# An attention kernel with a feed-forward behind it: the end of the sixth pair moved up, the first feed-forward begun five beats sooner, keys in blocks of 112

## The chip, the cores and the metric

The kernel runs on one core of a Trainium2 chip. The metric is the device time of one execution in microseconds. The median of three runs of the kernel before is 1040.24 us (1039.77 to 1040.38).

## The reference

Eight batches, twelve heads, 448 tokens, head size 64, all float32. Each head is normalised, attends over its 448 keys, and the heads of a token laid side by side (768 numbers) go through a feed-forward whose hidden layer is the largest of three products.

```
q_n = q / sqrt(mean(q*q) + 1e-6) * g_q          (k_n the same with g_k)
attn = softmax(q_n @ k_n.T / 8)
x = (attn @ v), heads side by side: 3584 x 768
h = max(x @ w1, x @ w2, x @ w3)                  768 x 768 each
out = h @ w_out                                  3584 x 768
```

## The kernel before, in words

Two heads make a pair, six pairs a batch, 48 pairs in all (numbered from 0 here, so that the sixth pair is pair 5). A pair has four chunks of queries: three of 128 rows for both heads, and a fourth of 64 rows for each head, which fill one PSUM bank together. So a pair has seven banks of scores.

**Two ways of doing a pair.** Pairs 0 to 5, all of batch 0, are done in float32 (`PLAIN = 6`): TensorE turns the exponentials by transposes against an identity (`turn_plain`, L627), ScalarE copies them out of PSUM (`keep_turned`), and the products with the values follow (`add_values`, L739). The sums of the softmax are turned and spread by sixteen small matmuls (`spread_sums`), copied by `keep_sums`, and the result is scaled by `scale_plain` and cut into two float16 parts by `finish`. From pair 6 on each number is two float16 parts; the weights of the softmax are cut by `upper_weights` (ScalarE, VectorE) and `lower_weights` (VectorE), and DMA does the turning (`turn_weights`).

**The order of the work is written out by hand.** A pair has twelve beats, and `beat(g, i)` (L993) issues what belongs to beat i while pair g is in its softmax. "Beat 6.4" is beat 4 of pair 6 in this text. Every engine does its instructions in the order of issue. While pair g is in its softmax, the end of the pair before (w = g - 1) is done: its sums, its products with the values, and `finish`. `later(n, work)` puts work off by n beats, to the end of that beat. Chunk c of a pair begins at beat 3c; from pair 6 on the scores of the next chunk are issued at beat 3c + 2, and VectorE's row maximum of a chunk stands ahead of `lower_weights` of the chunk before it.

**The feed-forward** of a batch is a generator (`ffn`, L874) of steps: a step of the first layer is three matmuls of 448 columns (L788), 108 of them a batch; a step of the second is three matmuls of 384 columns (L850), 36 or 48 a batch. `thirds` (L901) draws some two steps a beat, 24 a pair, from a queue of batches. Batch 0 enters the queue at beat 6.6, after its last pair; of its first two units only the first five of six steps are drawn at first, since the sixth needs the sixth pair. Later batches enter at beat 10 of the pair that follows them. If the queue is empty, no feed-forward is drawn.

**The weights** come as float32 in 24 blocks (18 of the first layer, 6 of the second). `prep_block` makes them ready: ScalarE works on the raw block (L186), VectorE takes three instructions (L194, L198, L203). A block of the first layer is due every 4 beats, one of the second every 8 (`BLOCK_BEATS`, L33); the next raw block of the second layer is loaded 9 beats after the block two ahead of it was begun.

**PSUM**: two buffers of two banks for scores, one bank for the products with the values, three banks (`ps_m`) that the turned tiles, the spread sums and the sums of the feed-forward share.

Of the kernel before, what the change touches and what calls it, by code (L numbers as in the profile page):

```python
# [13 lines left out]
ALU = mybir.AluOpType  # L14
AX = mybir.AxisListType.X

P = 128
# [12 lines left out]
LEAST = 2.0 ** -60  # L30


BLOCK_BEATS = (4, 8)  # L33


PLAIN = 6
# [6 lines left out]
def qknorm_attention_maxout_ffn_kernel(  # L43
# [35 lines left out]
    nc = tc.nc  # L79
    B, H, S, D = q.shape  # L80
    DM, DF = w1.shape
    DO = w_out.shape[1]
    NP = H // 2
# [5 lines left out]
    NH = 2  # L89
    HW = DO // NH  # L90
    LEFT = S - 3 * P
    G = B * NP
    HALVES = (slice(0, 64), slice(64, 128))
    TERMS = ((0, 0), (0, 1), (1, 0))
# [33 lines left out]
    ident = const.tile([P, P], F32, name="ident")  # L128
# [3 lines left out]
    ones_c = const.tile([P, 1], F32, name="ones_c")  # L132
# [34 lines left out]
    def row_largest(dst, src):  # L167
        nc.vector.tensor_reduce(dst, src, axis=AX, op=ALU.max, apply_absolute_value=True)
# [178 lines left out]
    v_tiles = {}  # L347

    def load_v(t):

        b, n = divmod(t, 2)
        vr = sb.tile([P, NP, 4, D], F32, name="vr", bufs=3)
        rows = v[b, NP * n:NP * (n + 1)]
        for u in range(3):
            nc.sync.dma_start(
                out=vr[:, :, u],
                in_=rows[:, u * P:(u + 1) * P].rearrange("h p d -> p h d"),
            )
        for half, part in zip(HALVES, (rows[:, 3 * P:S], rows[:, 0:LEFT])):
            nc.sync.dma_start(out=vr[half, :, 3], in_=part.rearrange("h p d -> p h d"))  # L360
        v_tiles[t] = vr

    def values_of(g):
        return v_tiles[g // 3][:, 2 * (g % 3):2 * (g % 3) + 2]
# [88 lines left out]
    def turn_whole(g, what):  # L453
# [10 lines left out]
        for to, of, rows in (  # L464
            (slice(0, LEFT), last, upper),
            (slice(LEFT + 3 * P, 512), last, lower),
# [22 lines left out]
    v_rows = {}  # L489
# [3 lines left out]
    def largest_v(t):  # L493
        b, n = divmod(t, 2)
        if b not in v_rows:
            v_rows[b] = sb.tile([P, 2], F32, name="v_rows", bufs=2)
        row_largest(
            v_rows[b][:, n:n + 1], v_tiles[t].rearrange("p h n d -> p (h n d)")
        )

    def bound_v(b):
        most = sb.tile([P, 1], F32, name="v_most", bufs=2)
        nc.vector.tensor_reduce(most, v_rows.pop(b), axis=AX, op=ALU.max)

        box = []


        def spread():
            box.append(ps_m.tile([P, 512], F32, name="most", tag="m"))
            nc.tensor.matmul(  # L510
                box[0][:, 0:1], ones_c.broadcast_to([P, P]), most, start=True, stop=True
            )

        def scale():
            nc.vector.tensor_scalar(
                out=v_down[:, b:b + 1], in0=box[0][:, 0:1], scalar1=LEAST, scalar2=1.0 / UP,
                op0=ALU.max, op1=ALU.mult,
            )
            nc.vector.reciprocal(v_up[:, b:b + 1], v_down[:, b:b + 1])

        later(2, spread)
        later(3, scale)
# [104 lines left out]
    def turn_plain(g, c):  # L627
        s = st[g]
        e = s.pop(("e", c))
        if c == 0:  # L630
            s["pt"] = sb.tile([P, 14, 512], F16, name="pt", bufs=2)
        s["turned"] = []
        s.pop(("sc", c))
        for h in range(banks(c)):
            turned = ps_m.tile([P, 512], F32, name="turned", tag="m")
            for u in range(3):
                block = e[:, h, u * P:(u + 1) * P]
                nc.tensor.transpose(turned[:, u * P:(u + 1) * P], block, ident)
            for first, rows in ((S - P, P), (S - LEFT, LEFT)):
                nc.tensor.transpose(turned[:rows, 3 * P:], e[:, h, first:S], ident)  # L640
            s["turned"].append(turned)

    def keep_turned(g, c):
        s = st[g]
        pt = pt_plain(s)
        turned = [t.rearrange("p (u q) -> p u q", u=4) for t in s.pop("turned")]
        for h in range(2):
            if c < 3:
                first = LEFT * h + c * P
                nc.scalar.copy(pt[:, h, :, first:first + P], turned[h])  # L650
            else:
                first = 0 if h else 3 * P
                nc.scalar.copy(
                    pt[:, h, :, first:first + LEFT], turned[0][:, :, HALVES[h]]
                )


# [81 lines left out]
    def add_values(g):  # L739
        s = st[g]  # L740
        av = ps_a.tile([P, 512], F32, name="av", tag="a")
        s["av"] = av
        if g < PLAIN:
            vr, pt = values_of(g), pt_plain(s)
            for u in range(4):
                rows = HALVES[0] if u == 3 else slice(0, P)
                for h, half in enumerate(HALVES):
                    nc.tensor.matmul(
                        av[half, :S], vr[rows, h, u], pt[rows, h, u],
                        start=u == 0, stop=u == 3,  # L750
                    )
            return
        vp, vs, pt = s["vp"], s["vs"], s["pt"]
        steps = [(part, u, u) for u in range(4) for part in range(2)]
        steps += [(2, u, 4 + u) for u in range(3)]
        for n, (part, u, block) in enumerate(steps):
            for h, half in enumerate(HALVES):
                values = vs[:, h, u] if part == 2 else vp[:, part, 4 * h + u]
                nc.tensor.matmul(  # L759
                    av[half, :S], values, pt[:, 7 * h + block, SHIFT[h]:SHIFT[h] + S],  # L760
                    start=n == 0, stop=n == len(steps) - 1,
                )
# [152 lines left out]
    for i, src in enumerate((g_q, g_k)):  # L915
        nc.scalar.dma_start(
            out=gains[:, i], in_=src.rearrange("(o d) -> o d", o=1).broadcast_to([P, D])
# [75 lines left out]
    def beat(g, i):  # L993
        w, n = g - 1, g + 2
# [19 lines left out]
        if part == 2:  # L1014
            if early:
                row_max(*divmod(k + 1, 4))
            elif k + 1 < 4 * G:
                scores(*divmod(k + 1, 4))
        if 0 <= w < PLAIN:
            if i == 1:  # L1020
                guard_sums(w)
            if i == 2:
                inverse_sums(w)
            if i == 5:
                spread_sums(w)
            if i == 6:
                keep_sums(w)
            if i == (8 if w < PLAIN else 9):
                scale_plain(w)
        if w >= 0 and i == (4 if w < PLAIN else 7):  # L1030
            add_values(w)
        thirds(THIRDS[i] + (len(queue) > 1 and i % 6 == 4))
        if w >= 0 and i == (9 if w < PLAIN else 10):
            finish(w, x_of[w // NP])
        if w >= 0 and g % NP == 0 and i == (6 if w < PLAIN else 10):
            queue.append(ffn(w // NP, x_of[w // NP]))

        if g + 1 < G:
# [55 lines left out]
        n_in = min(decoded[0], NFT * NJ)  # L1094
        due_at = BLOCK_BEATS[0] * n_in + BLOCK_BEATS[1] * (decoded[0] - n_in)
        if decoded[0] < len(blocks) and clock[0] > due_at:
# [44 lines left out]
```

## Time and profile before

| | before |
|---|---|
| median of three runs | 1040.24 us |
| the profiled execution | 1039.46 us |
| its span, first to last instruction | 1037.6 us |
| TensorE (PE) busy | 985.4 us, 95% |
| VectorE (DVE) busy | 709.3 us, 68% |
| ScalarE (ACT) busy | 637.1 us, 61% |
| GpSimd (POOL) busy | 614.2 us, 59% |
| mean granted TensorE clock | 0.984 of full speed |

The profile is of one execution. The shares of busy time are averages over stages that differ: the first 134 us (pairs 0 to 5), a stage in which the feed-forward sets in (to about 160 us), and the long rest. A stage's own rows say what it waits for. In a timeline row a bracket gives the idle time of the engine before the row and the work that ended it.

### The profile page before, as it was taken

To read this page: it belongs to the slowest core of one execution; us is meant where nothing else is said; L and a number is where in the kernel's file an instruction comes from. 1 tells how busy PE (TensorE), PEld (TensorE's weight loads), DVE (VectorE), ACT (ScalarE), POOL (GpSimd) and SP (SyncE) were. 2 spreads that over 40 slices of the span, in tenths; PEclk is the share of its full clock that TensorE was granted. 3 is DMA by queue.
4 is the path that set the end of the run, shared out by engine and by line. 5 is a ranking of instruction groups with operands and counts; after the bars stand their busy time and mean duration, and the time that the engine had idled before them with its cause. 6 is when DMAs were issued, how large, how long until landed. Compare 5 with 4: busy or idle time off the path is not lost.

```text
span 1037.6 us, 17168 instructions
## 1 busy us (share of the span) xinstructions
PE 985.4 (95%) x5850; PEld 527.5 (51%) x5850; DVE 709.3 (68%) x1316; ACT 637.1 (61%) x1437; POOL 614.2 (59%) x661
## 2 busy tenths in 40 slices
PE   5889869997899999999999999999999999999998
PEld 3555434444445555555555555555555555555555
DVE  4999989898676766777667757676677757760120
ACT  3697877757756666666666676666665766651111
POOL 5567878875766765767656666666675766400000
PEclk9899979999999999999999999999999999999999
DMA  7756669998999999999999899999999898762001
GB/s 176 190 159 170 158 162 205 186 177 139 211 180 176 164 185 204 172 176 155 211 169 185 156 202 196 175 169 182 191 172 174 168 202 148 139 99 62 1 1 61
DMA packets 524887, 166.17 MB, mean 160 GB/s; under 512 B 501120, under 2 KB 520576, under 8 KB 524800
## 3 DMA queue, kind: packets, MB, share of 16 engines
q1 hardware_dynamic: 461792, 149.09, 74.3%
q10 hardware_dynamic: 63008, 16.00, 8.8%
q8 instruction: 46, 0.75, 0.3%
q14 instruction: 41, 0.34, 0.1%
HBM read 53.54 MB, written 11.01 MB: 62 GB/s over the span
## 4 chain that ended last, share of the span: by engine, by line
PE 50%; DMA 1%; ACT 0%; SPq 0%; DVE 0%; issue 0%
PE acc L788 29%; PE acc L850 10%; PE av L759 5%; PE sc L579 5%; PE sc L586 1%; DMA pt<-pp 0%; DMA out_dram<-osb 0%; ACT osb L859 0%; SPq L732 0%; PE most L510 0%; DVE rs L700 0%; DVE rs L696 0%
## 5 line engine op out<-in xcount | busy, mean ns | idle before, releaser
L788 PE MATMUL acc<-xt,w_sb 128*128 128x448 f16 x2592 | 513.2, 353 | 0.0
L788 PEld LDWEIGHTS <-w_sb 128*128 128x128 f16 x2592 | 251.2, 98 | 242.7 <-issue 12.2
L617 ACT ACTIVATE sc<-sc,nm 128x448 f32<-128x448 f32 x294 | 178.8, 608 | 189.5 <-DVE nm L601 185.0
L601 DVE TENSOR_REDUCE nm<-sc 128x2 f32<-128x896 f32 x192 | 186.4, 971 | 97.8 <-PE sc L586 51.7
L703 ACT ACTIVATE pp<-sc,rs 128x448 f16<-128x448 f32 x294 | 172.8, 633 | 78.1 <-ACT sc L617 29.2
L713 DVE SCALAR_TENSOR_TENSOR pp<-sc,rs,pp 128x448 f16<-128x448 f32 x294 | 188.0, 675 | 4.9 <-ACT pp L703 4.9
L395 POOL TENSOR_TENSOR ri<-ri,half_neg 128x7 f32<-128x7 f32 x96 | 146.1, 1522 | 8.0
L850 PE MATMUL acc<-wo_sb,ht 128*128 128x384 f16 x864 | 147.9, 327 | 0.0
L429 POOL TENSOR_TENSOR kp<-kn,kp 128x448 f16<-128x448 f32 x42 | 44.3, 1056 | 168.6 <-ACT kp L423 159.0
L579 PE MATMUL sc<-kt,qt 128*128 128x448 f16 x504 | 117.5, 356 | 16.1 <-DVE pp L713 12.2
L850 PEld LDWEIGHTS <-ht 128*128 128x128 f16 x864 | 83.5, 98 | 59.6 <-issue 4.7
L579 PEld LDWEIGHTS <-qt 128*128 128x128 f16 x504 | 48.8, 98 | 63.6 <-issue 11.1
L759 PE MATMUL av<-pt,vp 128*64 128x448 f16 x672 | 72.6, 356 | 2.3 <-DMA pt<-pp 2.1
L817 POOL COPY hx<-ht 128x128 f16<-128x128 f16 x48 | 13.9, 289 | 93.6 <-DVE ht L812 89.3
L381 DVE TENSOR_REDUCE ss<-sq 128x7 f32<-128x448 f32 x96 | 57.7, 602 | 11.3 <-ACT sq L372 8.1
L541 POOL TENSOR_TENSOR vp<-vr,vp 128x512 f16<-128x512 f32 x42 | 49.9, 1189 | 22.6 <-ACT vp L535 22.6
L696 DVE TENSOR_SCALAR rs<-sc 128x2 f32<-128x2 f32 (+1 forms) x168 | 26.3, 157 | 52.5 <-ACT sc L617 52.5
L774 DVE SCALAR_TENSOR_TENSOR xt<-av,xt 128x448 f16<-128x448 f32 x42 | 26.2, 623 | 48.5 <-ACT xt L773 48.5
L802 DVE TENSOR_TENSOR m<-acc,m 128x448 f32<-128x448 f32 x48 | 29.6, 617 | 37.7 <-PE acc L788 37.5
L429 POOL TENSOR_TENSOR qp<-qn,qp 128x448 f16<-128x448 f32 x42 | 43.5, 1035 | 19.0 <-ACT qp L423 17.1
L759 PEld LDWEIGHTS <-vp 128*64 128x64 f16 x672 | 35.4, 109 | 36.6 <-issue 17.6
L808 ACT ACTIVATE ht<-acc 128x448 f16<-128x448 f32 x48 | 26.2, 546 | 41.8 <-DVE acc L802 41.8
(126 smaller groups left out, 1235.5 us busy)
## 6 DMA issues: line engine op xcount, KB each, us to landing
raw<-in_moe_w_dram SPq DMA_DIRECT2D x18, 768.0 KB, 4.6
kt<-kt SPq DMA_DIRECT2D x84, 112.0 KB, 2.4
vr<-in_v_dram SPq DMA_DIRECT2D x48, 192.0 KB, 4.2
out_dram<-osb SPq DMA_DIRECT2D x24, 384.0 KB, 3.4
kr<-in_k_dram ACTq DMA_DIRECT2D x34, 224.0 KB, 3.2
qr<-in_q_dram ACTq DMA_DIRECT2D x34, 224.0 KB, 4.5
raw<-in_moe_w_out_dram SPq DMA_DIRECT2D x6, 768.0 KB, 5.6
vs<-vp SPq DMA_DIRECT2D x84, 48.0 KB, 2.0
```

What stands on the lines that cost most here:

```text
L381: nc.vector.tensor_reduce(sums[g % 2][:, KQ[what]], sq, axis=AX, op=ALU.add)
L395: nc.gpsimd.tensor_tensor(out=ri, in0=ri, in1=half_neg[:, at], op=ALU.pow)
L429: nc.gpsimd.tensor_tensor(out=parts[:, :, 1], in0=n, in1=parts[:, :, 0], op=ALU.subtract)
L541: nc.gpsimd.tensor_tensor(out=vp[:, 1], in0=values_of(g).rearrange("p h n d -> p (h n) d"), in1=vp[:, 0], op=ALU.subtract,)
L579: nc.tensor.matmul(sc[:, h, :S], qt[:, 4 * h + c], kt[:, n, keys[h]], start=n == 0, stop=n == 1,)
L601: nc.vector.tensor_reduce(nm[:, :n], sc[:, :n, :S], axis=AX, op=ALU.max, negate=True)
L617: nc.scalar.activation(to, sc[:, h, :S], AF.Exp, bias=nm[:, h:h + 1], accum_out=total,)
L703: nc.scalar.activation(pp[:, h, 0], sc[:, h, :S], AF.Copy, scale=rs[:, h:h + 1])
L713: nc.vector.scalar_tensor_tensor(out=pp[:, h, 1], in0=sc[:, h, :S], scalar=rs[:, h:h + 1], in1=pp[:, h, 0], op0=ALU.mult, op1=ALU.subtract,)
L759: nc.tensor.matmul(av[half, :S], values, pt[:, 7 * h + block, SHIFT[h]:SHIFT[h] + S], start=n == 0, stop=n == len(steps) - 1,)
L788: nc.tensor.matmul(acc[:, :S], wt[:, wp, c], xs[c][:, xp], start=(c == 0 and n == 0), stop=(c == NCT - 1 and n == 2),)
L850: nc.tensor.matmul(acc[:, :HW], lhs, wo_sb[:, f, wp, half * HW:(half + 1) * HW], start=(f == 0 and n == 0), stop=(f == NFT - 1 and n == 2),)
```

## The change

The kernel after differs in three things.

- **Keys in blocks of 112** for batch 0: the 448 keys are four blocks of 112 instead of three of 128 and one of 64. A bank of exponentials is turned by four transposes instead of five; values of batch 0 are loaded in four transfers of 112 rows instead of five; the products with the values contract over 112 rows four times instead of 128 three times and 64 once.
- **The end of the sixth pair**, which is done in pair 6, is moved up: guarding the sums from beat 1 to 0, inverting them from 2 to 1, spreading them from 5 to 2, keeping them from 6 to 3, the products with the values from 4 to 2 (behind the spreading), scaling from 8 to 4, `finish` from 9 to 5. The other pairs keep their beats.
- **Batch 0 enters the feed-forward's queue** at beat 6.1 instead of 6.6, and blocks of the second layer are due every 7 beats instead of 8.

```
-BLOCK_BEATS = (4, 8)
+BLOCK_BEATS = (4, 7)
...
+    KEYS = S // 4
...
+        if b == 0:
+            for u in range(4):
+                nc.sync.dma_start(
+                    out=vr[:KEYS, :, u],
+                    in_=rows[:, u * KEYS:(u + 1) * KEYS].rearrange("h p d -> p h d"),
+                )
+            return
...
-            for u in range(3):
-                block = e[:, h, u * P:(u + 1) * P]
-                nc.tensor.transpose(turned[:, u * P:(u + 1) * P], block, ident)
-            for first, rows in ((S - P, P), (S - LEFT, LEFT)):
-                nc.tensor.transpose(turned[:rows, 3 * P:], e[:, h, first:S], ident)
+            for u in range(4):
+                nc.tensor.transpose(
+                    turned[:KEYS, u * P:(u + 1) * P], e[:, h, u * KEYS:(u + 1) * KEYS],
+                    ident,
+                )
...
-                rows = HALVES[0] if u == 3 else slice(0, P)
                 for h, half in enumerate(HALVES):
                     nc.tensor.matmul(
-                        av[half, :S], vr[rows, h, u], pt[rows, h, u],
+                        av[half, :S], vr[:KEYS, h, u], pt[:KEYS, h, u],
...
+        ends = w >= 0 and g % NP == 0
+        guard, spread, add, scale, end = (
+            (1, 5, 4, 8, 9) if w < PLAIN - 1 else (0, 2, 2, 4, 5) if w < PLAIN
+            else (0, 0, 7, 0, 10)
+        )
         if 0 <= w < PLAIN:
-            if i == 1:
+            if i == guard:
                 guard_sums(w)
-            if i == 2:
+            if i == guard + 1:
                 inverse_sums(w)
-            if i == 5:
+            if i == spread:
                 spread_sums(w)
-            if i == 6:
+            if i == spread + 1:
                 keep_sums(w)
-            if i == (8 if w < PLAIN else 9):
+            if i == scale:
                 scale_plain(w)
-        if w >= 0 and i == (4 if w < PLAIN else 7):
+        if w >= 0 and i == add:
             add_values(w)
         thirds(THIRDS[i] + (len(queue) > 1 and i % 6 == 4))
-        if w >= 0 and i == (9 if w < PLAIN else 10):
+        if w >= 0 and i == end:
             finish(w, x_of[w // NP])
-        if w >= 0 and g % NP == 0 and i == (6 if w < PLAIN else 10):
+        if ends and i == (1 if w < PLAIN else 10):
             queue.append(ffn(w // NP, x_of[w // NP]))
```

The reductions over the values of batch 0 and the copies of the turned tiles are cut to 112 partitions as well.

## Rows read from the trace of the kernel before

**Rows 1.** Page, part 1: engine, busy us (share of the span), instructions.

```profile
PE 985.4 (95%) x5850; PEld 527.5 (51%) x5850; DVE 709.3 (68%) x1316; ACT 637.1 (61%) x1437; POOL 614.2 (59%) x661
```

**Rows 2.** Chain that ended last, in order of time: start, us, what.

```profile
519.63 4.08 PE acc L788 x21
523.71 0.76 PE sc L579 x4
```

**Rows 3.** Windows, 10 us: length, busy (instructions) by engine, PEclk, DMA, GB/s.

```profile
110.00:120.00 10.00, 6.13 (x29) 3.54 (x29) 9.90 (x13) 8.88 (x20) 8.87 (x7) 0.83 0.68 162
...
130.00:140.00 10.00, 4.98 (x23) 3.18 (x23) 6.43 (x13) 8.48 (x20) 8.26 (x7) 0.83 0.62 161
...
140.00:150.00 10.00, 6.85 (x29) 3.64 (x25) 9.93 (x17) 5.33 (x10) 8.27 (x8) 0.69 0.74 170
```

**Rows 4.** Window of 18.6 us, one pair long, in the long rest.

```profile
310.97:329.57 18.60, 18.60 (x112) 9.52 (x110) 13.35 (x27) 12.51 (x30) 11.92 (x16) 1.00 1.02 170
```

**Rows 5.** Timeline of PE, two banks turned: start, us, line, tile, count.

```profile
117.44 0.90 PE L638 MATMUL turned<-ident,e 128*128 128x128 f32 x3
...
118.56 0.84 PE L638 MATMUL turned<-ident,e 128*128 128x128 f32 x3
```

**Rows 6.** Waits of VectorE, 20 to 140 us: total us, times, longest.

```profile
DVE top L156 <- PE marks L153: 2.3, 2, 1.4
```

**Rows 7.** Timeline of PE, pair 6 up to the first scores of pair 7.

```profile
138.29 0.35 PE L510 MATMUL most<-v_most,ones_c 128*128 128x1 f32 x2 [1.69 <-ACT qp L423]
...
138.57 3.57 PE L748 MATMUL av<-pt,vr 128*64 128x448 f32 x16
...
145.29 1.65 PE L579 MATMUL sc<-kt,qt 128*128 128x448 f16 x4 [3.15 <-DVE pp L713]
...
146.87 1.54 PE L673 MATMUL spread<-ident,sum 128*64 128x128 f32 x6
...
152.03 5.16 PE L788 MATMUL acc<-xt,w_sb 128*128 128x448 f16 x21
...
157.03 0.92 PE L579 MATMUL sc<-kt,qt 128*128 128x448 f16 x4
```

**Rows 8.** Timeline of PE, pair 5: first and last of four spreading groups.

```profile
123.16 0.87 PE L673 MATMUL spread<-ident,sum 128*64 128x128 f32 x6
...
125.01 0.32 PE L679 MATMUL spread<-ident,sum 64*64 64x64 f32 x2
```

**Rows 9.** Timeline of VectorE, pair 6.

```profile
139.91 0.20 DVE L664 RECIPROCAL sum<-sum 128x7 f32<-128x7 f32 x1 [0.67 <-ACT sum L660]
...
143.97 1.26 DVE L713 SCALAR_TENSOR_TENSOR pp<-sc,rs,pp 128x448 f16<-128x448 f32 x2
```

**Rows 10.** Timeline of PE, pair 12: scores of its chunks, then of pair 13.

```profile
263.96 0.92 PE L579 MATMUL sc<-kt,qt 128*128 128x448 f16 x4
...
268.62 0.92 PE L579 MATMUL sc<-kt,qt 128*128 128x448 f16 x4
...
272.44 0.92 PE L579 MATMUL sc<-kt,qt 128*128 128x448 f16 x4
...
275.73 0.57 PE L586 MATMUL sc<-kt,qt 128*64 128x448 f16 x4 [0.17 <-DVE pp L713]
...
278.95 0.92 PE L579 MATMUL sc<-kt,qt 128*128 128x448 f16 x4 [2.65 <-ACT sc L617]
```

**Rows 11.** Windows of 1 us.

```profile
144.00:145.00 1.00, 0.00 (x0) 0.00 (x0) 1.00 (x3) 0.88 (x3) 0.92 (x3) 0.50 0.85 172
...
277.00:278.00 1.00, 0.00 (x0) 0.00 (x0) 0.43 (x1) 1.00 (x4) 1.00 (x1) 1.00 1.06 336
```

**Rows 12.** Timeline of PE, 157 to 264 us: two of its waits.

```profile
167.58 0.92 PE L579 MATMUL sc<-kt,qt 128*128 128x448 f16 x4 [1.09 <-DVE pp L713]
...
254.17 0.93 PE L579 MATMUL sc<-kt,qt 128*128 128x448 f16 x4 [2.73 <-DVE pp L713]
```

**Rows 13.** Transfers of raw blocks of the second layer (L226), issue to landing.

```profile
DMA to landing us min/median/max: 4.4/5.6/6.3
```

More of the change, by code (lines that the diff above doesn't have):

```diff
@@ L353, in load_v @@
         rows = v[b, NP * n:NP * (n + 1)]
+        v_tiles[t] = vr
+        if b == 0:
[5 more added lines that the diff above has]
+            return
         for u in range(3):
@@ L360, in load_v @@
             nc.sync.dma_start(out=vr[half, :, 3], in_=part.rearrange("h p d -> p h d"))
-        v_tiles[t] = vr
     def values_of(g):
@@ L496, in largest_v @@
             v_rows[b] = sb.tile([P, 2], F32, name="v_rows", bufs=2)
+        rows = slice(0, P if b else KEYS)
         row_largest(
-            v_rows[b][:, n:n + 1], v_tiles[t].rearrange("p h n d -> p (h n d)")
+            v_rows[b][rows, n:n + 1], v_tiles[t][rows].rearrange("p h n d -> p (h n d)")
         )
@@ L502, in bound_v @@
         most = sb.tile([P, 1], F32, name="v_most", bufs=2)
-        nc.vector.tensor_reduce(most, v_rows.pop(b), axis=AX, op=ALU.max)
+        rows = P if b else KEYS
+        nc.vector.tensor_reduce(most[:rows], v_rows.pop(b)[:rows], axis=AX, op=ALU.max)
         box = []
@@ L510, in spread @@
             nc.tensor.matmul(
-                box[0][:, 0:1], ones_c.broadcast_to([P, P]), most, start=True, stop=True
+                box[0][:, 0:1], ones_c[:rows].broadcast_to([rows, P]), most[:rows],
+                start=True, stop=True,
             )
@@ L645, in keep_turned @@
         pt = pt_plain(s)
-        turned = [t.rearrange("p (u q) -> p u q", u=4) for t in s.pop("turned")]
+        turned = [t[:KEYS].rearrange("p (u q) -> p u q", u=4) for t in s.pop("turned")]
         for h in range(2):
@@ L649, in keep_turned @@
                 first = LEFT * h + c * P
-                nc.scalar.copy(pt[:, h, :, first:first + P], turned[h])
+                nc.scalar.copy(pt[:KEYS, h, :, first:first + P], turned[h])
             else:
@@ L653, in keep_turned @@
                 nc.scalar.copy(
-                    pt[:, h, :, first:first + LEFT], turned[0][:, :, HALVES[h]]
+                    pt[:KEYS, h, :, first:first + LEFT], turned[0][:, :, HALVES[h]]
                 )
```

## The prediction, made before the kernel after was built or run

> **What bounds the kernel now.** I read the page first: TensorE is busy 95% of the span [rows 1], so almost every wait that matters is one in front of it. The chain of waits then shows where it never waits: from 517 us to the end its pieces are TensorE's back to back, 21 matmuls of the first layer in 4.08 us (0.194 us each), scores in 0.76 us [rows 2]. The windows of one pair's length say the same from about 294 us on: 18.60 of 18.60 us busy [rows 4]. That part has the same matmuls in both kernels, so the change counts only by how much sooner its beginning is reached. The windows of 10 us show what stands ahead of it. In pairs 0 to 5 VectorE is the full engine (9.90 of 10 us, TensorE 6.13); where pair 6 begins neither is full (TensorE 4.98, VectorE 6.43), and the granted clock goes down to a mean of 0.69 [rows 3]. The timelines of TensorE and VectorE at pair 6 and pair 12 give the rest.
>
> **Keys in blocks of 112.** Removed: one transpose in each of 7 banks of 6 pairs, 42. At half clock two banks of five begin 1.12 us apart [rows 5], 0.22 us a transpose; at full clock I take half, 0.11 us. So 42 are 5 to 9 us of TensorE. But VectorE is the full engine there, and it waited for TensorE only at the reduction of the bound of a weight block, 2.3 us in two waits [rows 6]. Ahead of each stand some two turned banks at half clock, so I take 2 x 0.45 = **0.9 us**. Bounds: 0 (VectorE fills the time elsewhere) and the 9 us that they would be on the path. The copies on ScalarE keep their length along the free dimension, the products with the values keep eight matmuls of 448 columns, and SP issues two transfers fewer in all: nothing, each hidden in VectorE's full stretch; without that cover the copies would still cost the same as before.
>
> **The end of pair 5, and the feed-forward at beat 6.2.** Before, TensorE goes from the bound of the values at 138.29 to the first scores of pair 7 at 157.03, 18.74 us, with 3.15 us of waiting for `lower_weights` in front of the scores at 145.29, and half clock behind it [rows 7]. That wait ends last on VectorE, which itself waited 0.67 us for the guarded sums and then ran without a pause to 145.2 [rows 9]. After, TensorE's queue holds, from the same point: spreading 2.2 us (123.16 to 125.33 at full clock [rows 8]; 3.75 us before, at half clock, from 146.87), products with the values 3.6 us, the two small bounds 0.7 us, scores of two chunks 1.2 us, and 51 feed-forward matmuls instead of the 21 at 152.03 [rows 7] (ten steps of three drawn sooner), 51 x 0.194 = 9.9 us. Sum 17.6 us against 18.74: **1.1 us sooner, with 5.8 us more of the feed-forward done**. It holds if TensorE finds its inputs. The guarded sums need ScalarE a quarter of a microsecond behind the exponentials of pair 6; their inversion is 0.20 us on VectorE [rows 9], ahead of the bound of the values, so spreading can begin about where the bound began. Moved past the scores of chunk 2 of pair 6 are spreading, products and 18 matmuls: these scores come at about 147.5 instead of 145.29, and VectorE, whose work ahead of their row maximum grows by the moved scaling, is about as late. The cut of the result into two parts follows some four beats ahead of the step that reads it. Bounds: 2.8 us sooner (the 1.69 us in front of 138.29 go too), 3.9 us later (half clock for the 10 us for which it now lasts costs 5.0 us of work).
>
> **Blocks of the second layer every 7 beats.** The same three VectorE and one ScalarE instructions a block, all five beats sooner at the end, as the feed-forward that needs them: nothing in sum. Between 157 and 264 us TensorE waits six times on VectorE or ScalarE, from 1.09 us at 167.58 to 2.73 us at 254.17 [rows 12], 10.0 us together; I expect them moved, not gone, within 1.5 us either way. A raw block is now asked for 14 - 9 = 5 beats before ScalarE reads it instead of 7. A beat is 18.6 / 12 = 1.55 us, so 7.7 us against 4.4 to 6.3 us to landing [rows 13]: hidden; if not, ScalarE stands at that block with its exponentials behind it, a few tenths of a microsecond to 1.4 us each.
>
> **What comes late next: pair 12.** Batch 1 still enters the queue at beat 12.10. Counted through `thirds`, batch 0's feed-forward ended at beat 12.4 and now ends at 11.11, so twelve steps of the second layer leave beats 12.0 to 12.4, and eleven beats have no feed-forward. Only what these beats shrink by comes back of the 5.8 us. Before, the chunks of pair 12 begin 4.66, 3.82, 3.29 and 3.22 us apart, 14.99 us in all [rows 10]; the last two already had no feed-forward and did not shrink below 3.2, since each row maximum stands behind the exponentials, sums and weights of the chunk before. Four times 3.25 is 13.0, so at most 2.0 us are gained, at least none; the second interval (VectorE also reduces the values' bound and the sums of squares) shrinks little, and I take **1.0 us**.
>
> Sum: 0.9 + 1.1 + 1.0 = 3.0 us. The profiled execution took 1039.46 us, so 1036.5; the median of the runs is 0.8 us above it: **1037.2 us**. Two measurements of this kernel can be told apart from about 0.2%, 2.1 us.
>
> **Rival 1: TensorE was the limit after all, and all comes back.** If the six waits of 10.0 us shorten with a feed-forward that is ten steps ahead, or the transposes stood on the path at their 5 us, another 4 us go: 1033.2 us. For it: VectorE did wait for TensorE [rows 6]. Against it: VectorE's 9.90 of 10 us [rows 3]. Chance 0.14.
>
> **Rival 2: the clock falls at pair 12.** With no feed-forward TensorE has 0.76 us of scores in 3 to 4 us there. The rows: in the idle time at 144 us the granted clock is 0.50, the lower of the two levels (1.2 of 2.4 GHz), and it stayed there although TensorE was busy from 145.29 (the 21 matmuls at 152.03 took 5.16 us instead of 4.08 [rows 2, 7], so some 2.2 us of them, to about 154, were at half clock); in the idle time at 277 us, behind dense matmuls, it stayed 1.00 [rows 11]. The first idle time was longer and came behind another. Pair 12 would have two such times in a row. At half clock the products with the values take 2.2 us more, of which about 1.1 would show, and the first feed-forward matmuls of batch 1 lose up to 1.7 us: 1037.2 + 2.8 = 1040.0 us, no difference that can be measured. The Trainium skill, "TensorE: Matmul & The Clock Gate", section on HAM oscillation, says that gaps of idleness between bursts of matmuls bring the lower clock back again and again; by that rule an emptied queue is dear, and the row at 144 us agrees with it, the one at 277 us does not. Chance 0.21.
>
> **Rival 3: slower, the clock stays down in pair 6.** The place is 138 to 157 us. If spreading and the products with the values are too thin to hold the clock, as transposes and spreading were between 147 and 151 us, 10 us run at half clock: 3.9 us later instead of 1.1 sooner at the first scores of pair 7. VectorE then waits for the scores of chunk 2, which come at 152 or later, and the blocks of the second layer behind it are pushed back, some 1.5 us more: 1037.2 + 5.0 + 1.5 = 1043.7 us. Against it: the products alone, between idle times, ran at full clock from 138.57. It decides from about 4 us at half clock between 138 and 157 us. Chance 0.15.
>
> **The numbers.** Forecast 0.50, its own range 1035.0 to 1039.5; 0.36 of it lies more than 2.1 us below 1040.24, 0.14 within. With rival 1 faster is 0.50, with rival 2 the same is 0.35, slower is rival 3's 0.15. The range reaches into rival 1 and over rival 2: 1034.0 to 1041.5, which leaves out half of rival 1 and nearly all of rival 3.
>
> **What would show it.** Right: no drop of the granted clock between 138 and 157 us; no wait of 3 us in front of the scores of chunk 2 of pair 6; first scores of pair 7 about 2 us sooner (with the 0.9 us of pairs 0 to 5); pair 12 some 1 us shorter with idle times of 2 us or more in each chunk; the same 743 us or so behind it. Wrong: half clock in pair 12 or 13 (rival 2) or pair 6 (rival 3); waits between 157 and 264 us that add up to much else than 10 us (rival 1 if less); ScalarE waiting for raw blocks of the second layer.

## The result, and the profile of the kernel after

The kernel after took 1044.9 us (median of eight runs, 1042.17 to 1046.47) against 1040.31 us for the kernel before beside it (eight runs): a ratio of 1.0042, with a 95% interval of 1.0028 to 1.0055. It is slower by 4.6 us, and the forecast of 1037.2 us and its range (to 1041.5) are both missed. The profiled execution took 1045.47 us, its span is 1043.4 us, 5.8 us above that of before.

The page, part 1 (against [rows 1]) and the granted clock in 40 slices:

```profile
PE 988.5 (95%) x5808; PEld 527.1 (51%) x5808; DVE 709.9 (68%) x1316; ACT 637.6 (61%) x1437; POOL 617.3 (59%) x661
...
PEclk9899889999899999999999999999999999999999
```

TensorE has 42 instructions fewer and is 3.1 us longer busy: some of its work ran slower. The digits of the clock hardly show it, so the next view is the windows of 10 us, first of after (130 to 150 answers to [rows 3]):

```profile
130.00:140.00 10.00, 6.14 (x28) 4.13 (x27) 9.27 (x16) 9.85 (x22) 9.74 (x7) 0.63 0.77 189
140.00:150.00 10.00, 10.00 (x50) 4.68 (x49) 7.62 (x13) 4.96 (x10) 6.50 (x7) 0.86 0.85 165
170.00:180.00 10.00, 10.00 (x58) 4.65 (x57) 9.90 (x18) 6.28 (x14) 7.74 (x7) 0.83 1.02 181
190.00:200.00 10.00, 7.20 (x42) 3.27 (x42) 9.07 (x17) 6.10 (x14) 9.24 (x11) 0.83 0.80 140
...
270.00:280.00 10.00, 6.34 (x32) 2.94 (x31) 6.85 (x16) 7.87 (x19) 7.46 (x9) 0.80 0.92 185
```

and three of the same windows of before:

```profile
170.00:180.00 10.00, 9.69 (x63) 4.57 (x61) 9.36 (x17) 6.32 (x15) 7.32 (x7) 1.00 1.03 204
...
190.00:200.00 10.00, 9.70 (x63) 4.94 (x61) 8.31 (x17) 5.82 (x14) 7.75 (x9) 1.00 0.98 217
...
270.00:280.00 10.00, 7.18 (x54) 3.78 (x52) 7.64 (x18) 6.85 (x17) 7.03 (x8) 1.00 1.14 231
```

From 170 to 180 us TensorE is busy for all of 10 us in after and for 9.69 us in before, but at a clock of 0.83 it got through 58 matmuls (before: 63 at 1.00). Summed up, after has half clock (1.2 of 2.4 GHz) for 13.7 us between 160 and 265 us and 6.8 us between 265 and 300; before has none in either.

**Where the 5.8 us lie.** I measured every pair from the scores of the fourth chunk of the pair in front of it to those of its own fourth chunk, in one profile of each kernel. Pair 5's fourth chunk is reached 1.4 us later, pair 6 is as long as before, pairs 7 to 11 are 1.4, 2.8, -0.5, 3.4 and -1.4 us longer (5.8 together, before rounding), pair 12 is 0.3 longer, pair 13 and one pair far behind it are 0.8 us shorter each. Behind 300 us nothing else differs: pairs of 18.6 us, as in [rows 4]. So the loss is in pairs 7 to 11, which the prediction had put at nothing.

Pair 6 in TensorE's timeline of after, up to the first scores of pair 7 (against [rows 7]):

```profile
133.77 1.70 PE L590 MATMUL sc<-kt,qt 128*128 128x448 f16 x4
137.34 1.54 PE L684 MATMUL spread<-ident,sum 128*64 128x128 f32 x6 [1.87 <-DVE v_most L513]
...
141.09 4.07 PE L758 MATMUL av<-pt,vr 112*64 112x448 f32 x16
145.09 2.44 PE L798 MATMUL acc<-xt,w_sb 128*128 128x448 f16 x12
...
148.64 0.92 PE L590 MATMUL sc<-kt,qt 128*128 128x448 f16 x4
...
153.03 4.39 PE L798 MATMUL acc<-xt,w_sb 128*128 128x448 f16 x21
157.26 0.92 PE L590 MATMUL sc<-kt,qt 128*128 128x448 f16 x4
```

The wait of 3.15 us in front of the scores of chunk 2 is gone, as forecast, and TensorE works from 137.3 to 157.3 almost without a pause. But spreading (137.34 to 141.09, 3.75 us for an expected 2.2) ran at half clock, which lasted from 132.6 to 142.8 us. The first scores of pair 7 come at 157.26 (before: 157.03), with 30 feed-forward matmuls more done.

VectorE has a new wait in pair 6 of after, for TensorE's small matmul that spreads the bound of the values:

```profile
147.69 0.16 DVE L526 TENSOR_SCALAR v_down<-most 128x1 f32<-128x1 f32 x1 [1.78 <-PE most L520]
```

That matmul now stands on TensorE behind the products and four feed-forward steps, and VectorE stood 1.78 us for it.

The waits of TensorE of more than 0.9 us between 157 and 265 us in after (against [rows 12]):

```profile
168.97 0.93 PE L590 MATMUL sc<-kt,qt 128*128 128x448 f16 x4 [2.24 <-DVE pp L724]
...
192.80 0.93 PE L590 MATMUL sc<-kt,qt 128*128 128x448 f16 x4 [3.40 <-DVE pp L724]
...
220.43 0.38 PE L154 MATMUL marks<-ident,o_most 128*1 128x128 f32 x2 [1.90 <-DVE o_most L288]
...
243.59 0.57 PE L597 MATMUL sc<-kt,qt 128*64 128x448 f16 x4 [1.98 <-DVE pp L724]
...
250.87 0.92 PE L590 MATMUL sc<-kt,qt 128*128 128x448 f16 x4 [2.54 <-DVE pp L724]
```

They add up to 12.1 us, against 10.0 for the six in before, and behind four of them (170, 194, 221, 252 us) the clock is at half. TensorE's idle time grew by only 1.4 us between 160 and 265; the rest of what was lost is matmuls at the lower level of the clock. From the first scores of pair 7 to the fourth chunk of pair 13 (157.26 to 301.32, before 157.03 to 294.65) after needs 6.4 us more although 5.8 us of the work was already done: 12.2 us, of which 3.9 are more idle time (160 to 300) and the rest, some 8.3, is put down to work at half clock (20.5 us at half clock can lose up to 10.2).

**The longest new wait, on VectorE.** VectorE's timeline in pair 8 of after; the scores of chunk 1 were begun on TensorE at 185.08:

```profile
186.34 0.15 DVE L707 TENSOR_SCALAR rs<-sc 128x2 f32<-128x2 f32 x1
...
186.60 1.65 DVE L199 SCALAR_TENSOR_TENSOR wo_sb<-raw,wo_sb 128x768 uint32<-128x768 uint32 x1
188.17 0.60 DVE L389 TENSOR_REDUCE ss<-sq 128x7 f32<-128x448 f32 x1
188.70 1.86 DVE L204 SCALAR_TENSOR_TENSOR wo_sb<-raw,wo_sb 128x768 uint32<-128x768 uint32 x1
190.48 1.08 DVE L612 TENSOR_REDUCE nm<-sc 128x2 f32<-128x896 f32 x1
191.48 1.26 DVE L724 SCALAR_TENSOR_TENSOR pp<-sc,rs,pp 128x448 f16<-128x448 f32 x2
```

and in before, where these scores were begun at 182.88:

```profile
184.51 0.16 DVE L696 TENSOR_SCALAR rs<-sc 128x2 f32<-128x2 f32 x1 [1.68 <-ACT sc L617]
...
184.78 0.60 DVE L381 TENSOR_REDUCE ss<-sq 128x7 f32<-128x448 f32 x1
185.30 0.62 DVE L802 TENSOR_TENSOR acc<-acc,m 128x448 f32<-128x448 f32 x1
185.83 1.08 DVE L601 TENSOR_REDUCE nm<-sc 128x2 f32<-128x896 f32 x1
...
188.01 0.81 DVE L194 TENSOR_SCALAR wo_sb<-raw 128x768 uint32<-128x768 uint32 x1
...
189.52 0.95 DVE L198 SCALAR_TENSOR_TENSOR wo_sb<-raw,wo_sb 128x768 uint32<-128x768 uint32 x1
```

and the scores behind them on TensorE in before:

```profile
188.15 0.93 PE L579 MATMUL sc<-kt,qt 128*128 128x448 f16 x4 [0.93 <-DVE pp L713]
```

The last two instructions of a second-layer block are the same in both. In before they stand behind the row maximum of chunk 1 (blocks are due at beats 73, 81, 89, 97: the stages of the last at 8.3 to 8.5). In after the blocks are due at 73, 80, 87, 94; the stages of the last fall at 8.0 to 8.2, ahead of the row maximum, which is issued at 8.3. It starts 5.4 us behind its scores instead of 2.95, the next scores wait 3.40 us for `pp` (0.93 in before), and the clock falls.

### The profile page after: what moved, and what is told of

Its sections match the earlier page's. It is cut to its first block, busy times and chain, and to the rows that moved or that the text cites. A ratio compares the mean times of both kernels' runs of the same rounds, so it can differ in the third digit from the quotient of the medians.

```text
span 1043.4 us, 17085 instructions
## 1 busy us (share of the span) xinstructions
PE 988.5 (95%) x5808; PEld 527.1 (51%) x5808; DVE 709.9 (68%) x1316; ACT 637.6 (61%) x1437; POOL 617.3 (59%) x661
## 4 chain that ended last, share of the span: by engine, by line
PE 72%; DMA 1%; ACT 0%; DVE 0%; SPq 0%; issue 0%
PE acc L798 41%; PE acc L860 14%; PE av L769 8%; PE sc L590 8%; PE sc L597 1%; DMA pt<-pp 0%; DMA out_dram<-osb 0%; ACT sc L628 0%; DVE nm L612 0%; ACT osb L869 0%; SPq L743 0%; DVE ss L389 0%; PE most L520 0%; DVE rs L707 0%; DVE rs L711 0%
## 5 line engine op out<-in xcount | busy, mean ns | idle before, releaser
L552 POOL TENSOR_TENSOR vp<-vr,vp 128x512 f16<-128x512 f32 x42 | 48.9, 1164 | 22.6 <-ACT vp L546 22.6
L399 POOL TENSOR_SCALAR ri<-ss 128x7 f32<-128x7 f32 x54 | 17.0, 316 | 61.7 <-DVE ss L389 61.2
```

The source lines that it names most:

```text
L552: nc.gpsimd.tensor_tensor(out=vp[:, 1], in0=values_of(g).rearrange("p h n d -> p (h n) d"), in1=vp[:, 0], op=ALU.subtract,)
```

## The experiments

Changes of TensorE's order move small things all over the start, so each part was first tried alone. Times are medians over five to twelve runs, ratios against the kernel before on the same chip. "Pairs 7 to 11" is their length in the one profile of the kernel against that of before. Such a profile is one execution, not the median: e1's and e17's are the fastest of their twelve, those of e12 and e15 the slowest. In e13, whose code is that of before up to pair 12, the five pairs are 0.9 us longer, so a difference of that size can't be told from chance.

**One part alone (e1 to e3), and all but the sooner feed-forward (e4).**

e1: before with

```
-BLOCK_BEATS = (4, 8)
+BLOCK_BEATS = (4, 7)
```

> The kernel before with one change: blocks of the second layer every 7 beats. Theory A (the denser blocks put VectorE's three instructions a block in front of row maxima in pairs 7 to 11, and the longer waits of TensorE bring half clock): slower than before by 3 to 7 us, half clock in two or more places between 157 and 264 us. Theory B (the sooner feed-forward is the cause): within 1.5 us of before, at most one such place.

Measured: 1043.75 us, ratio 1.0020 (1.0008 to 1.0033); pairs 7 to 11 by 0, 4.1, -0.7, 3.0, -3.3, 3.0 together. The time lies between the two theories; half clock came in two places (189 and 240 us), as theory A said. VectorE in pair 8 shows the pattern of after; chunk 1's scores were begun at 180.66:

```profile
182.06 0.16 DVE L696 TENSOR_SCALAR rs<-sc 128x2 f32<-128x2 f32 x1 [1.67 <-ACT sc L617]
...
182.34 1.85 DVE L198 SCALAR_TENSOR_TENSOR wo_sb<-raw,wo_sb 128x768 uint32<-128x768 uint32 x1
...
185.17 1.33 DVE L203 SCALAR_TENSOR_TENSOR wo_sb<-raw,wo_sb 128x768 uint32<-128x768 uint32 x1
186.42 1.08 DVE L601 TENSOR_REDUCE nm<-sc 128x2 f32<-128x896 f32 x1
```

and TensorE the wait behind it:

```profile
188.74 1.44 PE L579 MATMUL sc<-kt,qt 128*128 128x448 f16 x4 [3.76 <-DVE pp L713]
```

What follows: seven beats by themselves cost some 2 us (0.8 to 3.4), and pair 8, where after loses time, shows how.

e2: before with the keys in four blocks of 112 (the three groups of lines of the diff that speak of `KEYS`).

> The kernel before with keys in blocks of 112 and nothing else. By the prediction's term 0.9 us faster, bounds 0 and 2.3. Both theories A and B: within 1.5 us of before, first scores of pair 7 at 155 to 157.5 us.

Measured: 1041.31 us, ratio 1.0005 (0.9990 to 1.0019). The window from 20 to 135 us of e2:

```profile
20.00:135.00 115.00, 95.87 (x536) 55.40 (x536) 109.56 (x135) 92.02 (x194) 86.54 (x65) 0.93 0.63 167
```

and of before:

```profile
20.00:135.00 115.00, 99.40 (x575) 59.57 (x576) 108.51 (x135) 91.13 (x193) 83.11 (x65) 0.91 0.64 169
```

TensorE is 3.5 us less busy and VectorE as full as ever (109.56 of 115): the transposes became idle time. No gain shows; the 0.9 us that were forecast lie at the edge of what the interval (1.0 us faster to 2.0 slower) leaves possible.

e3: before with the sixth pair's end moved up, the queue entered at 6.6 and blocks every eight beats as before.

```
+        ends = w >= 0 and g % NP == 0
+        guard, spread, add, scale, end = (
+            (1, 5, 4, 8, 9) if w < PLAIN - 1 else (0, 2, 2, 4, 5) if w < PLAIN
+            else (0, 0, 7, 0, 10)
+        )
```

> The kernel before with the sixth pair's end moved up, the feed-forward still at beat 6.6 and blocks every 8 beats. Theories A and B: within 2 us of before. If the moved end itself did harm (products and spreading in front of the scores of chunk 2 of pair 6), slower by 2 us or more with the first scores of pair 7 after 158.5 us.

Measured: 1042.41 us, ratio 1.0008 (0.9993 to 1.0023); pairs 7 to 11 by 1.3 us. The moved end alone neither gains nor loses what can be told.

e4: after with

```
-        if ends and i == (1 if w < PLAIN else 10):
+        if ends and i == (6 if w < PLAIN else 10):
```

> The kernel after with the feed-forward entering at beat 6.6 as before (end moved up, blocks every 7 beats, keys of 112 kept). Theory A: still slower than before by 3 us or more. Theory B: within 1.5 us of before, or faster.

Measured: 1044.74 us, ratio 1.0038 (1.0024 to 1.0052); pairs 7 to 11 by -0.7, 4.3, -0.7, 3.0, -3.2, 2.7 together. That is e1 + e2 + e3 (0.20 + 0.05 + 0.08 = 0.33%) within the intervals, and the kernel after (0.42%) is hardly above it. With blocks every seven beats, the 5.8 us of feed-forward drawn sooner bring nothing that can be told; with intervals of 0.14% either way a gain of more than some 2 us is excluded (estimate from the two intervals).

**Is it the blocks, the clock, or the sooner feed-forward? (e5 to e8)**

e5: after with the keys as before.

> The kernel after with the keys of batch 0 in blocks of 128 and 64 as before (end moved up, sooner feed-forward and blocks every 7 beats kept). Theory A (the denser blocks lengthen waits and bring half clock between 157 and 300 us): as slow as the kernel after, 3 to 6 us over before. Rival C (each part alone costs little and the three together meet badly; the keys' part shifts where the clock falls): half or less of it, 0 to 2.5 us over before.

Measured: 1046.04 us, ratio 1.0045 (1.0025 to 1.0065), at a mean clock over its runs of 0.983 (after 0.978, before on that chip 0.986). The keys have no part in it that shows; and a run can be slow at nearly the clock of before, so half clock is not the whole price.

e6 and e7: in after and in before, the scores of pairs 6 and later are issued behind the feed-forward steps of their beat instead of ahead of them, so that TensorE has work in front of the wait.

```
-            elif k + 1 < 4 * G:
-                scores(*divmod(k + 1, 4))
...
+        if part == 2 and not early and k + 1 < 4 * G:
+            scores(*divmod(k + 1, 4))
```

> The kernel after, with the scores of pairs 6 and on issued behind the feed-forward steps of their beat instead of ahead of them, so that TensorE has 1.1 us of work in front of each wait for the scores' buffer. Half-clock theory (what is lost is mostly work at half clock behind waits of 2 us or more): the waits of 2 to 3.4 us in front of scores shrink by about 1 us, half clock between 157 and 300 us falls from 20 us to under 8, and the time by 4 us or more against the kernel after, to before or below. If the waits only move and VectorE is the bound: the same as the kernel after, within 1.5 us.

> The kernel before with the same change of order as the last. Half-clock theory: waits of TensorE between 157 and 300 us of 15 us shrink to under 10, so 2 to 5 us faster than before. If VectorE is the bound there: within 1.5 us of before.

Measured: 1065.16 us (ratio 1.0228, 1.0207 to 1.0249) and 1055.3 us (1.0133, 1.0111 to 1.0154). Both lose over the whole length, also in the pairs behind 300 us that never waited: a later score makes all that follows on VectorE and ScalarE later. Idle time isn't removed by putting work in front of the instruction that others wait for. As a test of the clock it failed: half clock between 157 and 300 us fell from 20.5 to 6.8 us in e6, as expected, and the time still rose.

e8: after with blocks every eight beats; so that the weights are ready in time, the bound of the second layer takes one beat a step.

```
-BLOCK_BEATS = (4, 7)
+BLOCK_BEATS = (4, 8)
...
-        largest(most, scale, (1, 2, 2, 2))
+        largest(most, scale, (1, 1, 1, 1))
```

> The kernel after with blocks of the second layer every 8 beats again, and the chain behind the last of them (turn, reduce, spread, scale) one beat a step instead of two, so that the second layer's weights are ready as soon. Theory A: 2 us or more faster than the kernel after, within 2 us of before, half clock between 157 and 300 us down to 10 us or less. If the sooner feed-forward or the moved end is what costs: as slow as the kernel after, within 1.5 us.

Measured: 1045.86 us, ratio 1.0047 (1.0029 to 1.0066). Pair 8 is now 1.9 us shorter than before, but pairs 7, 9, 10, 11 are longer by 1.3, 1.1, 2.2, 1.2 (3.8 together). With the feed-forward drawn sooner, seven and eight beats are equally slow (1.0042 and 1.0047). So the sooner feed-forward has a price of its own, and the seven beats can't be held for the whole loss of the kernel after.

**Where within the pair? (e9 to e12)**

e9: after, queue entered at beat 6.3 instead of 6.1 (`i == (3 if w < PLAIN else 10)`).

> The kernel after with batch 0 entering the queue at beat 6.3 instead of 6.1: the first step is drawn six steps sooner than before instead of ten. A unit of the first layer is six steps, so the ends of units, with their work on VectorE and ScalarE, stand in the same beats of a pair as in the kernel before; entering at 6.1 moves them by four steps. Theory E (the position of the units' ends against the chunks costs, beside the cadence of the blocks): pairs 7 to 11 lose 2 to 3.5 us against before as with the blocks alone, instead of 5.8; time 1.5 to 3 us below the kernel after. Without it: as the kernel after, within 1.5 us.

Measured: 1045.32 us, ratio 1.0039 (1.0025 to 1.0054), as after.

e10: e9 with the two edits of e8.

> The same with blocks every 8 beats and the chain behind the last of them one beat a step (its split three beats sooner, as the feed-forward is). Theories A and E together (cadence and position of the units' ends): pairs 7 to 11 lose under 1.5 us against before, time within 1.5 us of before or up to 3 us below. If it is the split of the second layer's weights that meets the pair badly: 2 us or more over before, with the loss in pairs 10 and 11.

Measured: 1044.04 us, ratio 1.0024 (1.0012 to 1.0036), 2.5 us over before; pairs 7 to 11 by 4.2, 0.3, -0.3, 1.2, -0.7, 4.8 together. Neither expectation was met: it is slower than theories A and E allow, and the loss is in pair 7, not in pairs 10 and 11.

e11: before with the shorter bound of e8 alone, so that the cutting of the second layer's weights begins three beats sooner.

> The kernel before with the split of the second layer's weights three beats sooner, nothing else. Theory A (cadence) and theory E: within 1.5 us of before. Theory D (the place of the split costs): 2 us or more over before, lost in pairs 10 and 11.

Measured: 1040.27 us, ratio 0.9985 (0.9965 to 1.0006).

e12: before with blocks every seven beats, and a bound that takes five beats more (`largest(most, scale, (6, 2, 2, 2))`), so that the cutting keeps its place.

> The kernel before with blocks every 7 beats, but the split of the second layer's weights kept at its beats of before by a longer first step of the chain. Theory A (cadence): about 2 us over before, as with blocks of 7 beats alone, lost in pair 8. Theory D (the place of the split): within 1 us of before.

Measured: 1043.2 us, ratio 1.0012 (1.0000 to 1.0025); pair 8 longer by 2.6 us again, the five pairs 1.8 together. The time lies between the two theories. Cutting sooner costs nothing by itself (e11), with the cutting in its old place pair 8 is still longer (e12), and the beats at which the feed-forward's units end changed nothing that can be told (e9).

**Is the gain eaten where the next batch enters, and what does VectorE's share weigh? (e13 to e16)**

e13 and e14: in before and in after, batch 1's first units enter the queue in the beat of pair 12 in which batch 0's did in before, beat 6, so that the emptied beats are filled.

```
-        for unit in units[:2 if b == 0 else 0]:
+        for unit in units[:2 if b < 2 else 0]:
...
-        if w >= 0 and g % NP == 0 and i == (6 if w < PLAIN else 10):
+        if w >= 0 and g % NP == 0 and i == (6 if w < 2 * NP else 10):
```

> The kernel before with batch 1 entering the queue at beat 12.6 instead of 12.10, its first two units drawn to five of six steps at first, as batch 0's are. Nine steps (5.2 us of TensorE) go into beats that had none. If TensorE's idle time in pair 12 (about 3 us) is free for them: 2 to 4 us faster than before, kept to the end. If the beats are bound by the exponentials and their work is only pushed back: within 1 us of before.

> The same in the kernel after, which has no feed-forward in beats 12.0 to 12.10. If the emptied beats are what swallowed the 5.8 us drawn sooner (beats of fixed length, then half clock): 3 to 6 us faster than the kernel after. If not: less than 1.5 us.

Measured: 1040.79 us (ratio 1.0000, 0.9984 to 1.0016) and 1043.92 us (1.0030, 1.0012 to 1.0049). In e13 TensorE's idle time between 265 and 300 us falls from 4.2 to 1.3 us; then the emptied beats lie in pair 18, where batch 2 enters: the stretch from its fourth chunk to the next is 1.1 us shorter, but pair 13, now full, is 1.1 us longer. Nothing comes out. e14 is 1.2 us below after by the ratios, within the intervals and less than the 1.5 us that I had set as the limit.

e15 and e16: in before and in after, without the second and third VectorE instruction of the six second-layer blocks. These two kernels leave the output weights without their signs and last bits, so only their times are of use.

```
-        for stage in range(3):
+        for stage in range(3 if kind == "in" else 1):
```

> The kernel before without the second and third of VectorE's three instructions for each block of the second layer: twelve instructions of 0.95 to 1.8 us less, so w_out is left without its signs and last bits. If VectorE's order in front of the row maxima is the bound of pairs 7 to 9: 3 to 8 us faster than before. If not: within 1.5 us.

> The same left out of the kernel after. If the cadence of these blocks is what makes pairs 7 to 9 longer than before, the two kernels without the work differ by under 2 us, where the kernels with it differ by 4.4. If the sooner feed-forward and the moved end cost by themselves: 3 us or more between the two.

Measured: 1035.09 us (ratio 0.9950, 0.9934 to 0.9965) and 1038.13 us (0.9972, 0.9956 to 0.9988): by the ratios 5.2 us below before, and 7.3 us below after. VectorE's timeline in pair 8 of e16, with the scores of chunk 1 begun at 183.25:

```profile
184.36 0.14 DVE L707 TENSOR_SCALAR rs<-sc 128x2 f32<-128x2 f32 x1
...
184.62 0.60 DVE L389 TENSOR_REDUCE ss<-sq 128x7 f32<-128x448 f32 x1
185.13 1.08 DVE L612 TENSOR_REDUCE nm<-sc 128x2 f32<-128x896 f32 x1
```

The row maximum comes 1.9 us behind its scores (5.4 in after), and TensorE no longer waits for VectorE in that pair. The window from 157 to 265 us of after:

```profile
157.00:265.00 108.00, 95.94 (x528) 47.65 (x527) 91.40 (x163) 72.42 (x154) 74.00 (x76) 0.94 0.90 173
```

and of e16:

```profile
157.00:265.00 108.00, 100.48 (x585) 52.49 (x583) 83.65 (x162) 77.24 (x165) 74.38 (x80) 0.98 0.98 187
```

In the same 108 us TensorE gets 585 matmuls done instead of 528, at a clock of 0.98 instead of 0.94. Pairs 7 to 11 are 3.3 us shorter than before in e15 and 2.7 in e16: the gap of 5.8 us between the two kernels there is down to 0.6 in the profiles. The times don't bear that out: over twelve runs each on one chip e16 is still 3.0 us slower than e15 (0.22% by the ratios; after against before 0.42%). My expectation had set 3 us or more as the sign that the sooner feed-forward and the moved end cost by themselves. By the ratios the twelve instructions account for 2.1 us of the 4.4 between the kernels (7.3 against 5.2), as much as seven beats cost alone in e1; the rest isn't tied to them.

**Wider instead of closer, and what is harmless together (e17, e18).**

e17: before, blocks every 8.6 beats and the shorter bound of e8, which keeps the beats of the cutting (`BLOCK_BEATS = (4, 8.6)`).

> The kernel before with blocks of the second layer every 8.6 beats (by rounding 8 or 9), the chain behind the last of them one beat a step, so that its split stays at its beats. If a denser cadence costs because VectorE's instructions stand in front of row maxima, a thinner one gives: 1 to 2.5 us faster than before, pairs 7 to 9 shorter by about as much. If it is only the meeting of particular beats: anything within 2 us of before, with no such pattern.

Measured: 1043.91 us, ratio 1.0022 (1.0008 to 1.0037); pairs 7 to 11 by -0.2, 1.5, -1.4, 2.3, 1.5, 3.7 together (of which the 1.5 in pair 11 are one fall of the clock, shown in the last section). Blocks farther apart cost as much as blocks closer together, where I had expected 1 to 2.5 us less. That VectorE has too many of them in too short a time, which I had held since e1, is not borne out.

e18: e17 with the keys in blocks of 112 and batch 1 entered as in e13.

> The last kernel with keys in blocks of 112 and batch 1 entering at beat 12.6, the parts that cost nothing each for itself. If small gains add up: 2 to 4 us faster than before. If the head of the kernel only shifts its waits: within 1.5 us of before.

Measured: 1042.28 us, ratio 1.0009 (0.9995 to 1.0023). No version of these eighteen is clearly faster than before with all of its work; the nearest is e11.

## Why the prediction was wrong

**The step that failed** is the one on the blocks, with the stretch from 157 to 264 us behind it: "nothing in sum" for the blocks, and of TensorE's waits there "I expect them moved, not gone, within 1.5 us either way". It measured 5.8 us in pairs 7 to 11. The waits moved indeed, but they also grew (12.1 us for 10.0), and the clock fell behind them. Two changes have a price there, and the sum had neither.

The first is the blocks. Seven beats alone cost 0.20% or 2.1 us (e1), and pair 8 is longer by 2.6 to 5.5 us in each of the seven kernels that have them, all the work and the old place of the scores (after, e1, e4, e5, e9, e12, e14), by -1.9 to 1.5 us in those with 8 or 8.6. (With the scores issued later it is 1.0 in e6, with seven beats, and -2.1 in e7, with eight.) I counted each block's three instructions as so much VectorE time, which is the same wherever it stands (12.24 us in before, 12.25 in after for the ten long ones from 150 us on). I should have laid their beats, 73 + 7n, beside those of the row maxima. In pair 8, ahead of a row maximum, they delay the exponentials, the weights, the next scores, and TensorE with all that is queued there; behind it they take time in which the next scores waited only 0.93 us. e17 tells against the spacing as such, e15 and e16 that these instructions weigh 2.1 us more in after than in before.

The second is the feed-forward drawn sooner, whose price in later pairs I put at nothing without a reason. With eight beats it makes pairs 7 to 11 longer by 3.8 and 4.8 us (e8, e10), against 1.8 to 3.0 for seven beats without it (e1, e4, e12), 4.0 to 5.8 for both (after, e5, e9, e14) and 0.1 to 2.3 for neither (e2, e3, e11, e13). In the time the two do not add up: after (0.42%) lies within the intervals of e4 (0.38%), which lacks the sooner feed-forward, and of e8 (0.47%), which lacks the seven beats. How the sooner feed-forward brings its loss, and which of the meetings cost what in pairs 9 to 11, stays open.

**Keys:** 0.9 us was expected, nothing that can be told was found (e2). VectorE's waits for the marks, 2.3 us in before [rows 6], are 1.7 us in e2 and 2.4 in after.

**The end of pair 5:** 1.1 us sooner was expected with 5.8 us more done; the first scores of pair 7 came 0.2 us later, in that profile. But that profile had reached pair 5's fourth chunk 1.4 us later, and counted from there they came 1.2 us sooner (30.3 us for 31.5). The size is as forecast by luck: two errors cancel. Spreading and products were priced at full clock and took 2.0 us more (3.75 for 2.2, 4.07 for 3.6), and spreading began 10.4 us behind that chunk, where the bound of the values had begun 12.7 us behind it. The wait of 3.15 us went and the order held. Rival 3's own sign was there, 4.8 us at half clock between 138 and 157 us (10.2 in before), but not its price, since the clock was back from 143 us on; that its 1043.7 us lies near the measured time is luck.

Moreover the pair 6 that I subtracted from was a long one: over the profiles of eleven kernels without the sooner feed-forward pair 6 takes 22.3 to 25.6 us (before 25.6, mean 23.7), over seven with it 25.5 to 27.3 (mean 25.8); e6 and e7 are left out. So 5.8 us of the feed-forward were done for about 2 us there, and these 3.8 us didn't arrive: e4 and after differ by 0.04%.

**Pair 12:** 1.0 us was expected. From its first scores to those of pair 13, as the prediction counts, it is 0.3 us shorter; by the fourth chunks, as above, pair 12 is 0.3 us longer and pair 13 0.8 shorter. TensorE's timeline there (against [rows 10]):

```profile
273.85 0.93 PE L590 MATMUL sc<-kt,qt 128*128 128x448 f16 x4 [0.80 <-DVE pp L724]
277.99 1.67 PE L590 MATMUL sc<-kt,qt 128*128 128x448 f16 x4 [2.43 <-ACT sc L628]
279.65 3.30 PE L769 MATMUL av<-pt,vp 128*64 128x448 f16 x16
...
285.84 0.92 PE L590 MATMUL sc<-kt,qt 128*128 128x448 f16 x4 [1.95 <-ACT sc L628]
```

Its chunks begin 2.70, 4.14, 5.26 and 2.59 us apart, 14.69 in all for 14.99 before. Rival 2's mechanism occurred here, at a fraction of its 2.8 us (0.3 us gained for 1.0, and batch 1's first 21 matmuls took 4.14 us, at full clock): two waits of about 2 us follow on one another, and scores (1.67 us) and products (3.30) between them ran at half clock. The Trainium skill, "TensorE: Matmul & The Clock Gate", section "HAM oscillation", warns of gaps between bursts; pairs 8 and 12 of after agree with it. The waits of 2.50 and 2.73 us in before were gaps between bursts too, and no half clock followed them. e13 adds what no rival had: filling such beats gained nothing either; in its profile the work was then missing where the next batch enters.

**Right:** raw blocks of the second layer land in 4.9 to 6.5 us and ScalarE didn't wait for one; the long rest is unchanged. The sum of -3.0 us became +4.6, so 7.6 us are to be found: 5.8 in pairs 7 to 11, and the other 2 or so of the gains of keys, pair 6 and pair 12 that did not come. That second part is no larger than what one profile differs from the next.

## What to carry to other kernels

Where an order is written by hand, price a moved VectorE instruction by what stands right behind it in its queue at the new beat, not by its length: in pair 8 two such instructions behind a row maximum went with a wait of 0.93 us for the next scores, ahead of it with one of 3.40 us. Work drawn sooner from a queue gains only what the beats that it empties shrink by (0.3 us in pair 12 here), and it can cost in the pairs between: 5.8 us drawn sooner gave nothing that could be told. And take the length of a stage from several profiles before subtracting from it, and hold what one profile says against the medians of the runs, as e15 and e16 show.

## What was not expected of the hardware

**VectorE and GpSimd take turns.** An instruction of a block with 768 elements and two inputs in SBUF takes 0.94 to 0.96 us in some places and 1.65 and 1.86 us in pair 8 of after. GpSimd's timeline there:

```profile
185.96 1.48 POOL L552 TENSOR_TENSOR vp<-vr,vp 128x512 f16<-128x512 f32 x1
187.39 2.35 POOL L271 TENSOR_TENSOR w_sb<-w_sb 128x768 f16<-128x768 f32 x1
189.71 1.74 POOL L437 TENSOR_TENSOR qp<-qn,qp 128x448 f16<-128x448 f32 x1
```

VectorE's first (186.60) ends at 188.25, 0.81 us after GpSimd's L552 has ended at 187.44; GpSimd's L271 took 2.35 us (1.65 in before at 185.76, with no such VectorE instruction beside it) and ends at 189.74, and VectorE's second (188.70) ends at 190.56, 0.82 us after that. The Trainium skill, "SBUF — State Buffer", section "SBUF: two separate sides", says that a VectorE instruction with two SBUF inputs and a GpSimd instruction that reads SBUF share one pair of ports, that whichever comes first keeps it to its end, and that the other stands still; these rows agree with it. It adds some 1.6 us to what stood ahead of that row maximum. It was not tried by itself, and over all blocks the sum was equal in both kernels, so it makes one meeting dearer and not the kernel.

**The clock's answer to a wait varied.** In after, waits of 2.24 and 3.40 us were followed by half clock, in before waits of 2.50 and 2.73 us (the latter in [rows 12]) were not. The clearest case is the wait of 2.73 us in front of the scores of chunk 2 of pair 11. In e17 it is as long and stands behind the same 21 matmuls as in before:

```profile
255.06 1.68 PE L579 MATMUL sc<-kt,qt 128*128 128x448 f16 x4 [2.73 <-DVE pp L713]
```

There the clock went to half from 254.5 to 257.9 us, and the scores took 1.68 us instead of 0.93. So it did in e3, e13 and e18, with the same wait; in before and e2 it stayed full. With the fall pair 11 is 1.4 to 1.8 us longer than in before, without it (e2) it is equal. The same order of work can so differ from one execution to the next by one such fall.

**Two executions of the same instructions** reached pair 5's fourth chunk, some 127 us from the start, up to 2.9 us apart (e12 against before, whose code there is the same).
